# Banded attention and a top-1 mixture of experts in one program: loads, step order, routing order and the experts' branch are rearranged

## The chip, the core and the metric

The program runs on one core of one Trainium2 chip. A core has five engines with instruction queues of their own: PE multiplies matrices (its weight loads are shown as a row of their own, PEld), DVE, ACT and POOL do elementwise work, SP issues DMAs. Each runs its instructions in order; they wait for one another, and for transfers, by semaphores. Sixteen DMA engines move data between HBM and the core's SBUF, which has 128 partitions. The metric is device time in microseconds (us): the median over several runs of one execution of the whole program.

## What is computed

The inputs are q, k and v for 8 batches, 8 heads, 576 positions and 64 channels. Attention is banded: heads 0 to 3 see the last 32 positions, heads 4 to 7 see every fourth of the last 128. The result x (4608 tokens of 512) goes to a mixture of 8 experts, of which each token uses one:

```python
logits = x @ w_gate
e_idx = np.argmax(logits, axis=1)
gate_w = softmax(logits)[arange(N), e_idx]
eom = 1.0 / (1.0 + np.exp(-(x @ w_output_gate)))
for e in range(8):
    mask = e_idx == e
    h = np.maximum(x[mask] @ w1[e], 0.0)         # 512 -> 1024
    ye = h @ w2[e]                               # 1024 -> 512
    out[mask] = gate_w[mask, None] * eom[mask, e, None] * ye
```

How many tokens an expert gets is known only on the chip, once the logits are there.

## The kernel before

**Layout.** The positions of heads 4 to 7 are sorted by their rest modulo 4 on the host, so that both kinds of head see a band of 32 within blocks of 32. Two batches are one pair, a pair has nine steps, and a step works on 128 queries of all heads; there are 36 steps, g = 0 to 35. Buffers for q, k, v (`qb`, `kb`, `vb`) exist twice, for the even and the odd batch of a pair. `v2` is v moved on by one block, for the queries of even blocks. In `kb`, `vb` and `v2` the two heads that share a matmul lie in partitions 0 to 63 and 64 to 127, and zeros in the other half of each buffer keep them apart; the zeros are written once, by `clear`.

**One step.** `scores` adds the mask by a matmul and then 32 small matmuls into the PSUM tile `sp` (two buffers). `softmax` takes the maximum (L326), subtracts it (L330), both on DVE, takes exp on ACT (L336) and sums in halves on POOL (L341 to L347). `transpose_p` turns the weights on PE (L358) and ACT copies them to `pT` (L360). `values` multiplies by v (L370, 32 matmuls), `output` scales by the inverse sums into `x` on DVE (L392; four buffers) and SP writes `x` to the DRAM scratch `xs` in two or more DMAs (L402, L407). `transpose_x` turns `x` for the gate (L426) and ACT copies it to `xT` (L432, L435).

**Order.** The order on each engine is that of the program text (`manual_schedule`). Iteration g of the loop (L759) holds: transposed weights of step g-2, scores of g, x transposed of g-3, values of g-2, softmax of g, output of g-2. `load_qk` and `load_v` fetch the next pair's batches in pieces at fixed steps (table `loads`), all issued by SP, each to one half of the partitions; `v2` gets its upper 32 rows of each half by DMA (L285) and its lower 32 by a copy on DVE or ACT (`shift_v`, L290). Routing of a finished pair is spread over the next pair's steps by the tables `calm` and `brisk`: gate products, logits, argmax (`route_pick`), ranks, and one-hot matmuls into `perm`, from which come the lists of rows per expert.

**Experts.** Every expert has four 128-token tiles by default (`BASE`), expert 0 first three (`HEAD`), which are gathered from `xs` by indirect DMAs on POOL (L148; L162 in quarters). All values are split into a high and a low part of float32r, so that each product is three matmuls. Weights come as four 512 KB loads of each kind into the four `wraw` buffers (L110); ACT makes the high part (L128), DVE or POOL the low one (L132). For expert e the first products run over eight column blocks (`base_h`, L204, 12 matmuls each, then `relu` on ACT and DVE), the second over eight blocks and four tiles (`gemm2`, L835), then `finish` scales and scatters (L842 to L848). While expert 0's head runs, `during_first` and `during_second` do the last pair's routing. Tokens beyond four tiles are done after that, by one of five paths, chosen by a nest of compares of the count (`rest`, L1185 to L1193): nothing, up to 32 more, up to 128 more, up to 160 more, or two tiles more. In each path stands the second block of the next expert's first product (`fill`), as work for PE.

Of the kernel before, what the change touches and what calls it, by code (L numbers as in the profile page):

```python
# [7 lines left out]
F32 = mybir.dt.float32  # L8
# [7 lines left out]
PSUM = bass.MemoryType.PSUM  # L16

# [4 lines left out]
E = 8  # L22
# [24 lines left out]
def kernel(  # L47
# [21 lines left out]
    cnt = keep.tile([P, 2 * E + 3], I32, name="cnt")  # L69
# [155 lines left out]
    # ------------------------------------------------------------------ attention and routing  # L225
    with ExitStack() as actx:
# [30 lines left out]
        zeros = zero.broadcast_to([P, 2304])  # L257

        def clear(eng, t, c):
            r = slice(64 * (1 - c), 64 * (1 - c) + 64)  # L260
            v = t[r, c].rearrange("p a b -> p (a b)") if len(t.shape) == 4 else t[r, c].rearrange("p a b d -> p (a b d)")
            if eng is nc.scalar:
                eng.copy(out=v, in_=zeros[r])
            else:
                eng.memset(v, 0.0)

        def clear_first(z):
            for c in range(2):
                nc.gpsimd.memset(v2[z][64 * c + 32 : 64 * c + 64, c, :, 0], 0.0)

        def load_qk(b, j0, j1):
            z = b % 2
            nc.sync.dma_start(out=qb[z][:, :, 64 * j0 : 64 * j1], in_=qT[b, :, :, 64 * j0 : 64 * j1])
            for c in range(2):
                r = slice(64 * c, 64 * c + 64)
                nc.sync.dma_start(out=kb[z][r, c, j0:j1], in_=kT[b, r, j0:j1])

        def load_v(b, j0, j1):
            z = b % 2
            for c in range(2):  # L280
                r = slice(64 * c, 64 * c + 64)
                nc.sync.dma_start(out=vb[z][r, c, :, j0:j1], in_=vv[b, r, :, j0:j1])
                r = slice(64 * c + 32, 64 * c + 64)
                e1 = min(j1 + 1, 9)
                nc.sync.dma_start(out=v2[z][r, c, :, j0 + 1 : e1], in_=vv[b, r, :, j0 : e1 - 1])  # L285

        def shift_v(c, b, j0, j1):
            z = b % 2
            r = slice(64 * c, 64 * c + 32)
            (nc.vector.tensor_copy, nc.scalar.copy)[c](out=v2[z][r, c, :, j0:j1], in_=vb[z][r, c, :, j0:j1])  # L290
# [10 lines left out]

        def scores(g):
            var, subs = subs_of(g)
            sp = ps_s.tile([P, 512], F32, name="sp")
            nc.tensor.matmul(sp, lhsT=idb, rhs=mk[:, var], start=True, stop=False, skip_group_check=True)
# [15 lines left out]
            st[g, "s"] = sp  # L321

        def softmax(g):
# [7 lines left out]
                out=pt.rearrange("p (h k) -> p h k", h=H),  # L331
                in0=sp.rearrange("p (h k) -> p h k", h=H),
                in1=mx.unsqueeze(2).broadcast_to([P, H, 64]),
                op=ALU.subtract,
            )
            nc.scalar.activation(out=pt, in_=pt, func=AF.Exp, scale=1.0 / 8.0)  # L336
            sm = st[g, "sm"] = wk.tile([P, H], F32, name="sm", bufs=4)
            pv = pt.rearrange("p (h k) -> p h k", h=H)
            if g < last - 3 or g == last - 2:
                half = wk.tile([P, H, 32], F32, name="half", bufs=2)  # L340
                nc.gpsimd.tensor_tensor(out=half, in0=pv[:, :, 0:32], in1=pv[:, :, 32:64], op=ALU.add)  # L341
# [6 lines left out]
            st[g] = pt  # L348

        def late_sum(g):  # L350
            pv = st[g].rearrange("p (h k) -> p h k", h=H)
            nc.vector.tensor_reduce(out=st[g, "sm"], in_=pv, axis=AX.X, op=ALU.add)
# [33 lines left out]
        def output(g):  # L386
# [4 lines left out]
            x = wk.tile([P, DM], F32, name="x", bufs=4)  # L391
# [28 lines left out]
        def transpose_x(g):  # L420
# [7 lines left out]
            for p0 in range(0, P, n):  # L428
                b, i = subs[p0 // 32]
                o = (b % 2) * S  # L430
                s0 = 32 * i
# [20 lines left out]
        def gate_logits(pr, parts=(0, 4, 8)):  # L452
            lts = st[pr, "lt"]
            for c0 in parts:
                if c0 == 0:
                    R["spare"] = lts[0]
                    R["lg"] = rt.tile([P, NSTEP, 16], F32, name="lg")
# [917 lines left out]
```

## Time and profile before

| | |
|---|---|
| median of 3 runs | 714.92 us (713.82 to 715.13) |
| span of the profiled execution | 711.3 us |
| PE, DVE, ACT, POOL busy | 597.4, 351.5, 261.1, 372.3 us |
| mean granted TensorE clock | 0.940 |
| moved by DMA | 96.76 MB in 55784 packets |

The runs' time holds what lies around the span of the profile: 714.92 less 711.3 is 3.6 us. Attention takes the span up to some 204 us, expert 0 up to some 288, the other seven the rest. Busy time of an engine is the union of its instructions; DMA share is the mean busy share of the sixteen DMA engines, and can read above 1 where packets of one engine overlap. A row of a group has its busy time, the mean of one instruction, and the idle time of the engine before these instructions with what ended it.

### The profile page before, as it was taken

To read this page: it belongs to the slowest core of one execution; us is meant where nothing else is said; L and a number is where in the kernel's file an instruction comes from. 1 tells how busy PE (TensorE), PEld (TensorE's weight loads), DVE (VectorE), ACT (ScalarE), POOL (GpSimd) and SP (SyncE) were. 2 spreads that over 40 slices of the span, in tenths; PEclk is the share of its full clock that TensorE was granted. 3 is DMA by queue.
4 is the path that set the end of the run, shared out by engine and by line. 5 is a ranking of instruction groups with operands and counts; after the bars stand their busy time and mean duration, and the time that the engine had idled before them with its cause. 6 is when DMAs were issued, how large, how long until landed. Compare 5 with 4: busy or idle time off the path is not lost. (4 is left out here: it accounts for less than half of the span.)

```text
span 711.3 us, 13438 instructions
## 1 busy us (share of the span) xinstructions
PE 597.4 (84%) x5077; PEld 476.4 (67%) x5109; DVE 351.5 (49%) x620; ACT 261.1 (37%) x449; POOL 372.3 (52%) x497
## 2 busy tenths in 40 slices
PE   5685877877677799998599999499999959989992
PEld 4464655655456789786488788388778748858891
DVE  5453476594796574364175164256237417526020
ACT  4464555545563322343153243143234214324010
POOL 7753446474474376476475177277247647525110
PEclk8998998998899799999799999899999979999997
DMA  8999899889945342154155144244205415511010
GB/s 203 217 257 213 195 237 242 220 198 228 265 109 178 98 146 77 50 158 146 44 162 159 37 141 134 99 135 144 89 23 173 138 47 159 157 45 30 16 46 30
DMA packets 55784, 96.76 MB, mean 136 GB/s; under 512 B 10107, under 2 KB 40317, under 8 KB 55680
## 3 DMA queue, kind: packets, MB, share of 16 engines
q1 hardware_dynamic: 46800, 76.44, 40.8%
q0 software_dynamic: 8880, 18.91, 8.3%
q8 instruction: 68, 1.11, 0.7%
q14 instruction: 36, 0.29, 0.2%
HBM read 79.57 MB, written 19.27 MB: 139 GB/s over the span
## 5 line engine op out<-in xcount | busy, mean ns | idle before, releaser
L162 POOL DMA_INDIRECT sd<-xs,idx x112 | 130.4, 1164 | 34.0 <-issue 31.8
L204 PE MATMUL ph<-sc,w 128*128 128x512 f32 x480 | 115.8, 399 | 20.6 <-issue 17.4
L204 PEld LDWEIGHTS ph<-sc,w 128*128 128x128 f32 x480 | 91.6, 193 | 43.9 <-issue 20.6
L848 POOL DMA_INDIRECT out_dram<-yt,idx x39 | 38.6, 990 | 98.9 <-ACT yt L844 52.7
L162 POOL DMA_INDIRECT xg<-xs,idx x56 | 60.8, 1086 | 47.6 <-PE ph L204 22.6
L341 POOL TENSOR_TENSOR half<-pt 128x256 f32<-128x256 f32 x34 | 26.1, 767 | 67.4 <-ACT pt L336 67.0
L835 PE MATMUL y<-w,h 128*128 128x512 f32 x190 | 53.7, 390 | 0.0
L210 ACT ACTIVATE h<-ph 128x512 fp32r<-128x512 f32 (+1 forms) x48 | 28.1, 586 | 67.1 <-PE ph L204 62.1
L211 DVE SCALAR_TENSOR_TENSOR h<-ph,h 128x512 fp32r<-128x512 f32 (+1 forms) x48 | 32.3, 675 | 37.0 <-ACT h L210 36.9
L345 POOL TENSOR_TENSOR half<-half 128x128 f32<-128x128 f32 (+3 forms) x136 | 43.2, 318 | 10.7
L132 DVE TENSOR_TENSOR w<-wraw,w 128x1024 fp32r<-128x1024 f32 x36 | 44.0, 1227 | 8.1 <-ACT w L128 8.1
L392 DVE TENSOR_TENSOR x<-av,rs 128x512 f32<-128x512 f32 x36 | 24.8, 688 | 45.1 <-DMA xs<-x 23.8
L191 ACT CAST sc<-sd 128x512 fp32r<-128x512 f32 x28 | 17.4, 620 | 75.6 <-DVE sd L184 60.5
L204 PE MATMUL ph<-sc,sa 128*128 128x512 f32 (+1 forms) x132 | 35.8, 408 | 9.3 <-issue 8.2
L835 PE MATMUL z<-w,h 128*128 128x512 f32 x152 | 43.5, 389 | 0.0
L128 ACT CAST w<-wraw 128x1024 fp32r<-128x1024 f32 x40 | 41.6, 1044 | 0.0
L835 PEld LDWEIGHTS y<-w,h 128*128 128x128 f32 x190 | 35.5, 188 | 7.3
L370 PE MATMUL av<-sc,pT 128*32 128x128 f32 x288 | 26.7, 312 | 15.5 <-ACT pT L360 7.2
L426 PE MATMUL tp<-idn,x 128*128 128x128 f32 x144 | 24.3, 293 | 17.3 <-DVE x L392 15.0
L204 PEld LDWEIGHTS ph<-sc,sa 128*128 128x128 f32 x132 | 26.1, 205 | 14.4 <-issue 8.7
L326 DVE TENSOR_REDUCE mx<-sp 128x8 f32<-128x512 f32 x36 | 23.8, 662 | 21.6 <-PE sp L313 21.6
L426 PEld LDWEIGHTS tp<-idn,x 128*128 128x128 f32 x144 | 15.8, 145 | 27.9 <-DVE x L392 14.3
(284 smaller groups left out, 1344.5 us busy)
## 6 DMA issues: line engine op xcount, KB each, us to landing
wraw<-in_w_dram SPq DMA_DIRECT2D x64, 512.0 KB, 4.3
xs<-x SPq DMA_DIRECT2D x40, 128.0 KB, 5.8
vb<-in_vv_dram SPq DMA_DIRECT2D x8, 448.0 KB, 6.4
qb<-in_qT_dram SPq DMA_DIRECT2D x3, 896.0 KB, 9.8
kb<-in_kT_dram SPq DMA_DIRECT2D x6, 448.0 KB, 10.6
sb<-in_vv_dram SPq DMA_DIRECT2D x8, 320.0 KB, 5.0
sd<-in_qT_dram SPq DMA_DIRECT2D x4, 512.0 KB, 7.8
sa<-in_kT_dram SPq DMA_DIRECT2D x8, 256.0 KB, 6.9
```

Of the source, the lines that this page charges most:

```text
L128: nc.scalar.copy(out=W[e, kind][0][c], in_=raws[e, kind, c])
L132: sub.tensor_tensor(out=w[1][c], in0=raws.pop((e, kind, c)), in1=w[0][c], op=ALU.subtract)
L162: nc.gpsimd.indirect_dma_start(out=xg[j][:, P * a : P * a + P], out_offset=None, in_=xs4, in_offset=bass.IndirectOffsetOnAxis(ap=idx4[:, a ...
L204: nc.tensor.matmul(ph[:, 0:m], lhsT=part_of(w, a, o, P), rhs=x[:, c, 0:m], start=k == 0, stop=k == 3 * NC - 1)
L210: nc.scalar.activation(out=hh, in_=ph[:, 0:m], func=AF.Relu)
L211: nc.vector.scalar_tensor_tensor(out=hl, in0=ph[:, 0:m], scalar=0.0, in1=hh, op0=ALU.max, op1=ALU.subtract)
L341: nc.gpsimd.tensor_tensor(out=half, in0=pv[:, :, 0:32], in1=pv[:, :, 32:64], op=ALU.add)
L345: nc.gpsimd.tensor_tensor(out=dst, in0=half[:, :, 0:n], in1=half[:, :, n : 2 * n], op=ALU.add)
L370: nc.tensor.matmul(av[32 * a : 32 * a + 32, P * hp : P * hp + P], lhsT=pT[:, hp, 32 * a : 32 * a + 32], rhs=src[:, :, hp, i // 2, :], star ...
L426: nc.tensor.transpose(out=tp[:, c], in_=x[:, P * c : P * c + P], identity=idn)
L835: nc.tensor.matmul(y, lhsT=l[:, r], rhs=part_of(w, a, DM * fc, DM), start=fc == 0 and n == 0, stop=fc == NF - 1 and n == 2)
L848: put = nc.gpsimd.indirect_dma_start(out=out, out_offset=bass.IndirectOffsetOnAxis(ap=at.bitcast(U32), axis=0), in_=yt, in_offset=None, bo ...
```

## The change

**Attention, loads.** The two heads of a matmul now lie in alternate partitions: `lanes(c)` is every second partition, so that each DMA of 64 rows steps over all 128 partitions. Whole batches are loaded at once (`load_qk`, `load_vv`: 2 + 2 and 2 + 2 DMAs) instead of in pieces. The weights pt are kept in the matching interleaved order (`by_head`). `clear` now covers all 128 partitions, in two pieces for the first batch, and is left to DVE and POOL. For the first two pairs `v2` is made wholly on the core (`first_shift`: DVE one half of the partitions, ACT the other); for later pairs the upper half comes by DMA. At the start the first masks and k are issued by ACT, the rest by SP, cut to what the first steps need.

**Attention, order.** Iteration g now holds: transposed weights of g-2, mask of g, exp and sums of g-1, x transposed of g-4 (up to g = 27, then g-3), shifts, values and output of g-2, scores and maximum of g. Up to step 25 x lies in halves of the four `wraw` buffers (eight places), later in its own four. `transpose_x` copies in one piece, and the gate product reads the classes in strides (four products of 288 columns instead of 512, 512 and 128). The routing tables start earlier with the gates and end later. Ranks take 10 matmuls instead of 18, `route_spots` one instruction instead of nine. Low parts of expert 0's weights move from POOL to DVE.

**Experts.** In expert 0's head the last routing comes one block later, and its second weights are split on DVE in blocks 1 to 4. `choose` loads the number of an expert's path before its second product and announces the jump (`switch_hint`); the nest of compares becomes one jump through a table. Gathers go further ahead and are spread, the further tiles are prepared during the second product, two of each four blocks use other PSUM buffers, and the sums of a further tile lie in the tiles of the gathered rows, not in the output buffers.

```diff
+        def lanes(c, f0=0, f1=2):
+            return slice(64 * f0 + c, 64 * f1, 2)
+
+        def load_q(b, j0, j1):
             for c in range(2):
-                nc.gpsimd.memset(v2[z][64 * c + 32 : 64 * c + 64, c, :, 0], 0.0)
-
-        def load_qk(b, j0, j1):
+                s = slice(64 * j0, 64 * j1)
+                nc.sync.dma_start(out=qb[b % 2][lanes(c), :, s], in_=qT[b, rows_c(c), :, s])
+
+        def load_k(eng, b, j0, j1):
+            for c in range(2):
+                eng.dma_start(out=kb[b % 2][lanes(c), c, j0:j1], in_=kT[b, rows_c(c), j0:j1])
+
+        def load_qk(b):
+            load_q(b, 0, 9)
+            load_k(nc.sync, b, 0, 9)
+
+        def load_vv(b):
+            for c in range(2):
+                nc.sync.dma_start(out=vb[b % 2][lanes(c), c], in_=vv[b, rows_c(c)])
+                nc.sync.dma_start(out=v2[b % 2][lanes(c, 1), c, :, 1:9], in_=vv[b, rows_c(c, 1), :, 0:8])
+
+        def first_shift(f, b, j0, j1):
+            z = b % 2
+            j0, j1 = max(j0 - f, 0), j1 - f
+            r = slice(64 * f, 64 * f + 64)
             for c in range(2):
-                r = slice(64 * c, 64 * c + 64)
-                nc.sync.dma_start(out=kb[z][r, c, j0:j1], in_=kT[b, r, j0:j1])
+                (nc.vector.tensor_copy, nc.scalar.copy)[f](
+                    out=v2[z][r, c, :, j0 + f : j1 + f], in_=vb[z][r, c, :, j0:j1]
+                )
...
+            if g >= 26:
+                x = wk.tile([P, DM], F32, name="x", bufs=4)
+            else:
+                if g % 2 == 0:
+                    st["rows"] = stage.tile([P, 1024], F32, name="wraw")
+                x = st["rows"][:, DM * (g % 2) : DM * (g % 2) + DM]
...
+        load_k(nc.scalar, 0, 0, 2)
+        nc.scalar.activation(out=warm, in_=zero, func=AF.Exp)
...
+        loads = {4: 0, 8: 1}
...
         for g in range(last + 1):
             if g >= 2:
                 transpose_p(g - 2)
-                inverse(g - 2)
+            if g < last:
+                mask(g)
+            if g >= 1:
+                softmax(g - 1)
+            if 4 <= g <= hurry:
+                transpose_x(g - 4)
+            if g >= hurry:
+                transpose_x(g - 3)
             shift(1, g)
...
             if g >= 2:
                 values(g - 2)
-            routing(g, "ahead")
+                inverse(g - 2)
+                output(g - 2)
+                load(g - 2, load_vv if g > NSTEP + 2 else whole_v)
             if g < last:
-                softmax(g)
-            if g >= 2:
-                output(g - 2)
-                load(g - 2, load_v)
...
+                scores(g)
+                shifted(g)
...
+    def choose(e):
+        flag[e] = nc.values_load(cnt[0:1, 2 * E + 3 + e : 2 * E + 4 + e], min_val=0, max_val=len(PATHS))
+        flag[e, "hint"] = tc.switch_hint({t: flag[e] for t in ENGINES}, len(PATHS) + 1, f"paths{e}")
...
-        elif k == 1:
+        elif k == 2:
             rank_products(pr)
...
-            split_w(0, 1, k, nc.gpsimd)
+        if 0 < k < 5:
+            split_w(0, 1, k - 1)
...
+    for n in tc.Switch(flag["rare"], 2, flag["rare", "hint"]):
+        products1(1, 1, *X, BASE * P, ph, (1, 2, 3))
+        if n:
+            repair()
...
-            h.append(base_h(e, fc, X, BASE * P))
+            h.append(base_h(e, fc, X, BASE * P, ph=bank(ps_x, "tpx") if fc % 4 > 1 else None))
             if fc == 2:
-                gather4(e, 4)
-                gather4(e, 5)
-                next_gathers(e + 1)
+                rows_of(e + 1, *((2, 3) if e > 1 else range(BASE)))
+                rows_of(e, 4, 5)
...
-            if fc >= 6:
-                prep4(fc - 2, *xx, fc - 6)
+        choose(e)
...
+            if fc in (4, 5):
+                prep4(fc, *xx, fc - 4)
+            if fc == 5:
+                rows_of(e + 2, 0, 1)
...
-        rest([
-            ((BASE + 1) * P + 32, two),
-            ((BASE + 1) * P, lambda: extra(e, BASE, xx, 1, 1, fill)),
-            (BASE * P + 32, lambda: extra(e, BASE, xx, 1, 0, fill)),
-            (BASE * P, lambda: extra(e, BASE, xx, 0, 1, fill)),
-            (0, nothing),
-        ])
+        bodies = [
+            nothing,
+            lambda: extra(e, BASE, xx, 0, 1, fill),
+            lambda: extra(e, BASE, xx, 1, 0, fill),
+            lambda: extra(e, BASE, xx, 1, 1, fill),
+            two,
+        ]
+        for n in tc.Switch(flag[e], len(bodies), flag[e, "hint"]):
+            bodies[n]()
```

More of the change, by code (lines that the diff above doesn't have):

```diff
@@ L443, in gate_products @@
+                nc.scalar.copy(out=xT[:, :, o : o + n], in_=tp[:, :, p0 : p0 + n])
+        def gate_products(pr, parts=range(4)):
+            if (pr, "lt") not in st:
+                st[pr, "lt"] = rt.tile([P, 2 * S], F32, name="lt")
+            m = S // 2
+            for k in parts:
+                o = S * (k // 2)
+                i0 = m // NCLS * (k % 2)
                 gp = ps_t.tile([P, 512], F32, name="tp")
                 for c in range(NC):
+                    by_class = _free(xT, 2 * S * c + o + i0, [[1, m // NCLS], [CLS, NCLS]])
@@ L897, with rows_of @@
     pr = NPAIR - 1
-    def next_gathers(e):
+    def rows_of(e, *js):
         if e < E:
-            for j in range(BASE):
+            for j in js:
                 gather4(e, j)
```

343 lines of the change are left out of this document (176 added, 167 removed).

## The prediction

> **What bounds the kernel now.** I read the page first, then engine busy time by stage, then PE's waits in each stage, then the DMA rate in single stretches, then the branches.
>
> ```profile
> span 711.3 us, 13438 instructions
> DMA  8999899889945342154155144244205415511010
> ```
>
> Forty slices of 17.8 us: the DMA engines are at eight tenths and more in the first eleven, the attention, and mostly below five later. The stages, with columns us, then PE, PEld, DVE, ACT, POOL busy, PE clock, DMA share, GB/s:
>
> ```profile
> 0.00:204.00 204.00, 147.62 (x2759) 111.25 (x2791) 122.56 (x279) 104.88 (x210) 114.23 (x268) 0.91 0.94 223
> 204.00:288.00 84.00, 73.95 (x523) 63.81 (x524) 52.88 (x119) 28.22 (x54) 47.63 (x41) 0.94 0.35 112
> 288.00:711.00 423.00, 375.78 (x1796) 301.31 (x1794) 176.05 (x223) 128.03 (x186) 210.45 (x189) 0.96 0.32 99
> ```
>
> There are three limits. In attention PE is idle for 56.4 of 204 us while DMA is at 0.94: transfers set the pace. In the other two stages DMA is at a third, and PE is busy 73.95 of 84 and 375.78 of 423: PE sets the pace, and only its idle time can be won. What ends the waits in attention, for PE and then for DVE and ACT (us in total, times, longest):
>
> ```profile
> PE tp L426 <- DVE x L392: 12.9, 9, 2.7
> PE sp L313 <- DMA sa<-in_kT_dram: 6.3, 2, 5.6
> PE av L370 <- DMA sb<-in_vv_dram: 5.1, 1, 5.1
> DVE x L392 <- DMA xs<-x: 23.8, 9, 5.6
> ACT sc L290 <- DMA sb<-in_vv_dram: 21.1, 5, 7.6
> ```
>
> PE's longest wait is for x, and x waits for one of its four places, whose write to DRAM stands in the same queue as the loads. So this too is a transfer that is late.
>
> Why are the transfers slow at a share of 0.94? One stretch shows it. SP issued a q load (all 128 partitions), then the k pair (64 neighbouring partitions each), and the two stretches are those in which first q, then k moves; the third holds v loads, 64 neighbouring partitions too:
>
> ```profile
> 65.82 0.60 SPq L273 DMA_DIRECT2D qb<-in_qT_dram  x1
> 66.46 1.27 SPq L276 DMA_DIRECT2D kb<-in_kT_dram  x2
> ...
> 69.50:72.50 3.00, 2.64 (x40) 2.25 (x44) 0.63 (x2) 1.63 (x2) 2.44 (x8) 0.50 1.13 323
> 73.00:76.00 3.00, 2.86 (x48) 1.72 (x41) 1.08 (x2) 2.11 (x5) 0.04 (x1) 1.00 0.96 186
> 86.00:88.00 2.00, 1.85 (x40) 1.49 (x35) 1.47 (x5) 1.60 (x4) 1.00 (x2) 1.00 1.11 200
> ```
>
> With all DMA engines busy, q moves at 323 GB/s, k at 186, v at 200: a load into half of the partitions goes at some 0.6 of the rate.
>
> **Attention, transfers.** Per batch q, k and v have 1152 KB each and the upper half of v2 512 KB (64 rows of 4 x 8 x 64 floats). Over eight batches k, v and v2 are 23.1 MB; at 193 GB/s, between 186 and 200, that is 120 us of the DMA time, which is 0.94 x 204 = 192 us. q is 9.4 MB at 323, 29 us. The other 43 us are x, masks and expert 0's weights. The change steps every load over all 128 partitions and drops v2's load for four batches: 21.0 MB are left in place of 23.1. No row shows a load with a step between partitions. Below, its rate is that of half the partitions (193), above, that of q (323). I take q's, since a stepped load reaches from partition 0 to 127 as q does: 21.0 MB in 65 us, and 43 + 29 + 65 = 137 us in place of 192.
>
> The Trainium skill has this as a rule ("SBUF — State Buffer", section Door 1: The DMA port swizzle): 64 neighbouring partitions reach 8 of the 16 ports, about half of the bandwidth. The measured 186 to 200 against 323 agree. The same section says that only a transfer spanning all 128 partitions hits all ports; if "spanning" meant touching each of them, the lanes would gain nothing, and that is the first rival.
>
> **Attention, PE.** With transfers at 137, PE's 147.6 us are the longest sum, so PE becomes the bound. How full can PE get here? The fullest stretches of ten us, and a middling one:
>
> ```profile
> 80.00:90.00 10.00, 9.22 (x196) 7.44 (x198) 7.55 (x16) 5.08 (x12) 4.81 (x14) 1.00 0.76 164
> 170.00:180.00 10.00, 8.76 (x189) 7.22 (x183) 5.91 (x16) 2.30 (x5) 2.43 (x8) 1.00 0.69 176
> ```
>
> Where DMA is at 0.7 to 0.8, PE is busy for 0.88 to 0.92. I take the lower: 147.6 / 0.88 = 168 us, 36 less than 204; bounds 0.92 (160, a gain of 44) and 0.80 (184, a gain of 20). The reordering is costed inside this term: x one step later and with eight places takes away the 23.8 and the 12.9, exp of the step before takes ACT's and DVE's time off the way to the next scores. Its cover is gone if another engine exceeds PE, so I add up DVE and ACT from these rows (a shift on each; the subtraction that writes pt; the one-hot rows; a low part on DVE; x's copies and a copy of a whole tile on ACT):
>
> ```profile
> L290 DVE COPY sc<-sb x8: 671/744/1508, 17.3 to 166.1; 32x1024 f32<-32x1024 f32 x4, 32x1280 f32<-32x1280 f32 x4
> L290 ACT COPY sc<-sb x8: 1041/1148/1255, 18.5 to 164.4; 32x1024 f32<-32x1024 f32 x4, 32x1280 f32<-32x1280 f32 x4
> L330 DVE TENSOR_TENSOR pt<-sp,mx 128x512 f32<-128x512 f32 x36 | 24.9, 692 | 3.1
> L567 DVE TENSOR_SCALAR ohp<-cb,pos 128x128 bf16<-128x128 bf16 x36 | 12.5, 417 | 0.0
> L132 DVE TENSOR_TENSOR w<-wraw,w 128x1024 fp32r<-128x1024 f32 x36 | 44.0, 1227 | 8.1 <-ACT w L128 8.1
> L435 ACT COPY xT<-tp 128x256 f32<-128x256 f32 (+7 forms) x64 | 24.1, 444 | 0.0
> L432 ACT COPY xT<-tp 128x256 f32<-128x256 f32 (+1 forms) x40 | 14.4, 359 | 17.8 <-PE tp L426 17.3
> L360 ACT COPY pT<-tp 128x512 f32<-128x512 f32 x36 | 20.8, 578 | 10.5 <-PE tp L358 10.2
> ```
>
> A batch's shift is two such copies per engine. DVE: four batches with twice the shift, + 4 x 1.5; two batches given to ACT, - 2 x 1.5; three times nine one-hot rows (27 x 0.417 = 11.3) become three instructions of up to 3.8, no gain below and 11 above, I take - 5; three low parts from POOL, + 3.7. That is 122.6 + 2 = 124 of 168. ACT: 24.1 + 14.4 become 40 copies of 0.58, - 15; shifts + 4 x 2.3 and + 2 x 2.3, + 14; at the start the k and mask DMAs in ACT's queue (0.6 each, eight) replace its three clears. So ACT stays near 105. Each stays under PE, but in single steps with routing DVE will not (its mean is 124 / 36 = 3.4 us a step, PE's 147.6 / 36 = 4.1); the step of slack that x gets takes such a burst. The interleaved write of pt and the strided read of the gate product have no row; at nothing they cost 0, at twice the time (L330's group is 24.9 us, all on DVE) DVE would reach 149 and stand beside PE. I take 0, since the same elements are read.
>
> **Expert 0.** What PE waits for between 204 and 288:
>
> ```profile
> PE tp L504 <- DVE oh L495: 4.0, 1, 4.0
> PE perm L573 <- DVE ohp L567: 3.4, 2, 2.1
> PE tp L426 <- DVE x L392: 2.1, 1, 2.1
> PE tp L176 <- DVE sc L180: 1.7, 1, 1.7
> ```
>
> That is 11.2 us. Ranks one block later put 12 more matmuls (some 2.3 us by the blocks' pace) ahead of the 4.0; fewer one-hot instructions shorten the way to the 3.4, but three of the four low parts at 1.23 now stand on DVE in front of it. Neither of the other two is touched. I take - 5, between 0 and - 9.
>
> **Experts 1 to 7.** PE's waits after 288, the branch instructions of the nest, and one of the three long waits:
>
> ```profile
> PE ph L204 <- issue: 25.6, 3, 9.2
> PE ph L204 <- ACT sc L191: 3.2, 3, 1.3
> PE y L1053 <- DMA out_dram<-yt,idx: 1.9, 1, 1.9
> PE y L1043 <- ACT sa L210: 1.6, 1, 1.6
> PE ph L204 <- DVE sc L192: 0.7, 3, 0.2
> ...
> L1190 PEldq COMPARE_BRANCH  x26: 70/340/4714, 334.6 to 692.7; - x26
> L1190 ACTq COMPARE_BRANCH  x26: 38/45/55, 337.6 to 697.1; - x26
> ...
> 334.09 2.81 PE L204 MATMUL ph<-sc,w 128*128 128x512 f32 x11 [0.22 <-DVE sc L192]
> 346.06 0.79 PE L204 MATMUL ph<-sc,w 128*128 128x512 f32 x1 [9.16 <-issue]
> ```
>
> Three experts have no further tokens and pass the whole nest; there PE stands still for 25.6 us, waiting for nothing but its own sequencer, since its branches take up to 4.7 us and ACT's 0.05. A long one costs between 9.16 / 3 = 3.1 and 4.7. One jump in place of four compares removes 25.6. If it is announced in time it costs what a short branch does, 0.07 to 0.34, under the 2.81 of queued matmuls. If not, up to 4.7 once on entering and once on leaving, less the same cover: up to 1.9 each. I take 0.4 for each of seven experts, 3 in all. On the other engines, whose branches are short now, the table could bring such jumps: at most 9.4 us after each expert's output. Behind them wait the next relu and low parts; PE has four blocks of twelve matmuls (some 2.9 each, 11 in all) before it needs a PSUM buffer back, as two more buffers are used. So: nothing, and with that cover gone up to 6 us each. The 1.9 and 1.6 are waits for output buffers and for an ACT sum in further tiles, which now lie elsewhere: I take both off. In sum - 25.6 - 3.5 + 3 = - 26.
>
> Here the skill ("Runtime: NRT & Kernel Launch", section Instruction fetch mechanics) says that a taken branch out of a small window of 256-instruction blocks forces a fetch, and it knows no announcement. The 4.7 on PE against 0.05 on ACT agrees; by that rule alone the jump would stay a fetch, which is the second rival.
>
> The start of the next expert waits 3.2 + 0.7 for rows' preparation, late because 24 gathers stand in a row on POOL. They are spread and the further tiles' eight go behind the next expert's: - 3.5, between 0 and - 3.9.
>
> **Sum.** 711.3 - 36 - 5 - 26 - 3.5 = 640.8. The runs' median stands 3.6 above the span, so 644.4.
>
> **Rivals.** First, the stepped loads are no faster: 43 + 29 + 21.0 MB / 193 (109) = 181, at the same share of 0.94 it is 193 us, a gain of 11 in place of 36: 669. For it: no row has such a step. Against it: 323 beside 186 within seven us of the trace. Second, the announcement doesn't help: 1.9 twice on the seven, less the 3 counted, + 12 at most by half covers, + 24 with none of it hidden: 656 to 668. With both, 681. Third, slower than before: the stepped loads are slower than those into neighbours, q among them, which loses its full load. All loads are then 30.4 MB, and the other terms give back 34.5; the kernel is slower once (43 + 30.4 MB / rate) / 0.94 exceeds 238.5, which is from 168 GB/s down. At 150 it is 43 + 203 = 246, a stage of 261: 711.3 + 57 - 34.5 + 3.6 = 737. For it: q's two DMAs now have half of the rows each. Against it: no full stretch above is under 186, and whole batches make longer rows.
>
> **How the numbers follow.** Forecast 0.62 (own range 630 to 660), first rival 0.16, second 0.14, third 0.05, anything that leaves no difference 0.01, other mishaps 0.02 that still are faster. The range reaches down to 628 (PE at 0.92, 9 in expert 0) and up to 678, so that the first two rivals and nearly their sum are in. A measurement here tells 0.2% from nothing, that is 1.4 us. Faster 0.94, same 0.01, slower 0.05.
>
> **What will show it.** k loads at 300 GB/s and more with DMA full; the last scores starting before 170 us; PE's waits for x and DVE's for xs gone; no PE wait "issue" above 2 us after 288; PE near 0.9 busy in attention. The forecast is wrong if attention still has DMA at 0.94, or if DVE's busy share there passes PE's.

## The result and the profile after

The changed kernel takes 629.45 us (median, 626.08 to 631.82) against 714.75 us before (713.82 to 715.13), a ratio of 0.8803 with the interval 0.8767 to 0.8839. The forecast was 644.4, with an own range of 630 to 660; the measured time lies just below that and inside the whole range of 628 to 678. The profiled execution took 631.7 us and has a span of 629.9.

From the page after: the span, the engines' busy time, and the row of 40 slices (now 15.7 us each) for the granted clock.

```profile
span 629.9 us, 13742 instructions
PE 580.8 (92%) x5084; PEld 468.2 (74%) x5109; DVE 353.2 (56%) x621; ACT 256.6 (41%) x416; POOL 364.9 (58%) x488
PEclk9889999999999999999999999999999999999995
```

The same two rows for PE and its clock from the page before:

```profile
PE 597.4 (84%) x5077; PEld 476.4 (67%) x5109; DVE 351.5 (49%) x620; ACT 261.1 (37%) x449; POOL 372.3 (52%) x497
PEclk8998998998899799999799999899999979999997
```

PE does nearly the same matmuls (5077 and 5084 records, and 5109 weight loads in both), yet it is busy for 16.6 us less. The clock row goes with it: before, it has a 7 or an 8 at several places all along the span; after, it has hardly one behind the third slice. The forecast had held PE's work constant.

Engine busy time by stage shows both parts. Columns: us, then PE, PEld, DVE, ACT, POOL busy, PE clock, DMA share, GB/s. First before: attention, head of expert 0, experts 1 to 7, and then one of the three long waits, cut into the wait, the time behind it and the time after that.

```profile
0.00:211.50 211.50, 152.99 (x2848) 115.44 (x2880) 129.25 (x287) 110.63 (x222) 120.68 (x273) 0.91 0.91 217
211.50:265.00 53.50, 45.59 (x295) 38.82 (x291) 35.45 (x90) 16.56 (x30) 27.22 (x21) 0.90 0.43 139
288.00:697.00 409.00, 375.71 (x1796) 301.31 (x1794) 176.05 (x223) 127.34 (x185) 209.46 (x188) 0.97 0.33 102
337.00:346.00 9.00, 0.00 (x0) 0.00 (x0) 0.69 (x1) 0.59 (x1) 1.78 (x2) 0.62 0.25 91
346.00:349.30 3.30, 3.24 (x8) 2.56 (x9) 0.00 (x0) 0.00 (x0) 1.86 (x2) 0.50 0.10 25
349.30:353.00 3.70, 3.70 (x18) 3.05 (x17) 0.69 (x1) 0.60 (x1) 2.79 (x4) 0.99 0.13 35
```

Then after: the same three stages, and a stretch in which a stepped k load moves.

```profile
0.00:176.00 176.00, 148.54 (x2871) 115.38 (x2896) 134.06 (x288) 106.16 (x192) 119.31 (x268) 0.97 0.79 249
176.00:218.90 42.90, 41.19 (x279) 34.64 (x275) 33.11 (x90) 16.06 (x26) 18.04 (x17) 1.00 0.52 169
241.00:614.00 373.00, 368.86 (x1799) 297.92 (x1797) 175.53 (x223) 128.08 (x185) 212.50 (x189) 1.00 0.36 114
53.00:56.00 3.00, 2.93 (x70) 2.55 (x73) 2.46 (x6) 2.62 (x6) 1.67 (x4) 1.00 1.00 346
```

Behind the wait of 9 us PE works for 3.3 us at a clock of 0.50: eight matmuls where the next 3.7 us hold eighteen. Such a stall costs its length and some of the work behind it. The two parts by stage, from these rows (idle is the stretch less PE's busy time):

| | PE idle | PE busy |
|---|---|---|
| attention | 58.5 to 27.5, -31.0 | -4.5 |
| expert 0's head | 7.9 to 1.7, -6.2 | -4.4 |
| experts 1 to 7 | 33.3 to 4.1, -29.2 | -6.9 |

That is 66.4 us of idle time and 15.7 us of busy time. By exact bounds (first product of expert 0, of its two further tiles, of expert 1, last matmul) the stages went from 211.5, 53.5, 22.8, 409.3 and 14.2 us to 176.0, 42.9, 22.5, 372.8 and 15.7. These stage times are used for all experiments below. One execution of each kernel was profiled: in the six profiles whose attention is as changed it takes 170.1 to 176.0 us, the kernel after being the longest, so differences of up to 6 us in that stage say little.

What PE still waits for in attention after (us in total, times, longest), and what DVE waits for:

```profile
PE tp L461 <- DVE x L427: 6.0, 5, 2.0
PE sp L336 <- issue: 4.1, 2, 2.7
...
DVE wraw L427 <- PE av L400: 7.9, 4, 5.9
DVE rs L414 <- POOL sm L378: 7.6, 9, 1.4
```

DVE's 23.8 us for a place of x are gone, and of ACT's 21.1 for the v loads into `sb` 5.0 are left. The rest is spread over many short waits. In experts 1 to 7 no wait of PE is above 1.2:

```profile
PE tpx L206 <- DVE el L213: 1.2, 1, 1.2
...
PE tpx L206 <- issue: 0.8, 1, 0.8
```

### The profile page after: what moved, and what is told of

Read it like the earlier page. It is cut to its first block, busy times and chain, and to the rows that moved or that the text cites. A ratio compares the mean times of both kernels' runs of the same rounds, so it can differ in the third digit from the quotient of the medians.

```text
span 629.9 us, 13742 instructions
## 1 busy us (share of the span) xinstructions
PE 580.8 (92%) x5084; PEld 468.2 (74%) x5109; DVE 353.2 (56%) x621; ACT 256.6 (41%) x416; POOL 364.9 (58%) x488
## 3 DMA queue, kind: packets, MB, share of 16 engines
q1 hardware_dynamic: 30352, 72.90, 36.5%
## 5 line engine op out<-in xcount | busy, mean ns | idle before, releaser
L206 PE MATMUL tpx<-sc,w 128*128 128x512 f32 x240 | 56.7, 391 | 2.7 <-DVEq L1285 1.0
L206 PE MATMUL ph<-sc,w 128*128 128x512 f32 x240 | 57.6, 391 | 0.0
L206 PEld LDWEIGHTS tpx<-sc,w 128*128 128x128 f32 x240 | 44.7, 188 | 13.6 <-PE ph L206 2.6
L206 PEld LDWEIGHTS ph<-sc,w 128*128 128x128 f32 x240 | 44.7, 188 | 10.7 <-issue 1.7
L370 POOL TENSOR_TENSOR half<-pt 128x256 f32<-128x256 f32 x34 | 29.5, 868 | 27.3 <-ACT pt L365 26.4
L899 PEld LDWEIGHTS y<-w,h 128*128 128x128 f32 x190 | 35.4, 188 | 9.1 <-issue 1.8
L193 ACT CAST sc<-sd 128x512 fp32r<-128x512 f32 x28 | 17.4, 621 | 52.3 <-issue 33.3
L213 DVE SCALAR_TENSOR_TENSOR h<-tpx,h 128x512 fp32r<-128x512 f32 x28 | 19.3, 691 | 26.1 <-ACT h L212 26.1
L899 PEld LDWEIGHTS z<-w,h 128*128 128x128 f32 x152 | 28.5, 188 | 5.9
L365 ACT ACTIVATE pt<-pt 128x512 f32<-128x512 f32 x36 | 22.7, 631 | 24.6 <-DVE pt L355 15.5
L212 ACT ACTIVATE h<-tpx 128x512 fp32r<-128x512 f32 x28 | 16.8, 599 | 38.0 <-PE tpx L206 35.6
L194 DVE TENSOR_TENSOR sc<-sd,sc 128x512 fp32r<-128x512 f32 x28 | 19.4, 693 | 20.3 <-ACT sc L193 20.3
L390 ACT COPY pT<-tp 128x512 f32<-128x512 f32 x36 | 21.1, 587 | 18.5 <-PE tp L388 18.4
```

The source lines that it names most:

```text
L194: nc.vector.tensor_tensor(out=view(xl[:, :, r]), in0=tv, in1=view(xh[:, :, r]), op=ALU.subtract)
L206: nc.tensor.matmul(ph[:, 0:m], lhsT=part_of(w, a, o, P), rhs=x[:, c, 0:m], start=k == 0, stop=k == 3 * NC - 1)
L213: nc.vector.scalar_tensor_tensor(out=hl, in0=ph[:, 0:m], scalar=0.0, in1=hh, op0=ALU.max, op1=ALU.subtract)
L370: nc.gpsimd.tensor_tensor(out=half.rearrange("p (h c) k -> p h c k", c=2), in0=pv[:, :, :, 0:32], in1=pv[:, :, :, 32:64], op=ALU.add)
L390: nc.scalar.copy(out=pT, in_=tp)
L899: nc.tensor.matmul(y, lhsT=l[:, r], rhs=part_of(w, a, DM * fc, DM), start=fc == 0 and n == 0, stop=fc == NF - 1 and n == 2)
```

## The experiments

Theory A behind the forecast, now with the clock added: attention was paced by loads at some 0.6 of the rate, the experts by the nest's branches, and each long idle stretch also costs PE some work at half the clock. The rivals are named at each run. Unless said otherwise an edit is made to the changed kernel.

### The nest of compares back

```diff
-        flag[e, "hint"] = tc.switch_hint({t: flag[e] for t in ENGINES}, len(PATHS) + 1, f"paths{e}")
...
-        for n in tc.Switch(flag[e], len(bodies), flag[e, "hint"]):
-            bodies[n]()
+        def rest(n):
+            if n == 0:
+                bodies[0]()
+                return
+            with tc.If(flag[e] > n - 1) as more:
+                bodies[n]()
+            with more.Else():
+                rest(n - 1)
+        rest(len(bodies) - 1)
```

> The changed kernel, with the nest of compares in place of the announced jump. In the trace of the kernel before, PE stood idle 25.6 + 1.9 + 1.6 us after its branches, and half-clock windows lay over the time after each of the three long ones. Theory A (idle time and the clock after it): the 29 us come back and some 5 us more of PE time at half clock, time 660 to 665, three half-clock windows among the experts. Theory B (idle time alone, as the prediction had it): 26 us, time 655 to 658, clock among the experts as now.

Measured: 664.63 us (661.87 to 665.26), ratio 0.9309 (0.9272 to 0.9345). The experts' stage takes 408.2 us, 35.4 more than in the changed kernel. Its row, PE's first waits in it, and the nest's branches on PE (count, then shortest, median and longest in ns):

```profile
238.00:646.00 408.00, 380.21 (x1797) 304.95 (x1795) 175.76 (x223) 127.63 (x185) 209.06 (x188) 0.96 0.33 102
...
PE ph L206 <- issue: 18.7, 3, 6.6
PE y L1129 <- issue: 4.0, 2, 3.2
...
L1289 PEldq COMPARE_BRANCH  x26: 70/3094/3832, 281.6 to 641.8; - x26
```

Idle time is 27.8 us against 4.1, so 23.7 more, and PE's busy time is 11.4 higher at a clock of 0.96: 35.1 in sum. The nest alone thus carries nearly the whole gain of this stage (36.5), and a third of that is clock. Theory A had the total, but with more idle time (29) and less of the clock (5). What the rows of the next experts and the buffers gave, costed at 3.5 each in the forecast, this run does not separate: its stage is only 1.1 us shorter than that of the kernel before, with 5.5 us less idle time and 4.5 more of busy time.

### The jump without its announcement

```diff
-        flag[e, "hint"] = tc.switch_hint({t: flag[e] for t in ENGINES}, len(PATHS) + 1, f"paths{e}")
...
-        for n in tc.Switch(flag[e], len(bodies), flag[e, "hint"]):
+        for n in tc.Switch(flag[e], len(bodies)):
```

> The jump through the table stays, its announcement goes (for experts 1 to 7). Theory A (the announcement brings the code in time): PE is held up at each jump by a fetch of 3.1 to 4.7 us less some 2.8 us of queued matmuls, on entering and perhaps on leaving: 8 to 24 us more, 637 to 653. Theory B (one jump instead of four compares is the whole gain): no more than 2 us longer than the changed kernel, 628 to 632.

Measured: 628.53 us (627.73 to 630.46), ratio 0.8809 (0.8771 to 0.8847): no difference from the changed kernel. PE's jumps with the announcement, and then without it:

```profile
L1448 PEldq COMPARE_BRANCH  x16: 293/320/4100, 241.0 to 609.9; - x16
```

```profile
L1447 PEldq COMPARE_BRANCH  x16: 309/2382/3992, 236.4 to 605.9; - x16
...
236.00:609.00 373.00, 368.54 (x1797) 298.05 (x1796) 175.26 (x223) 127.36 (x185) 212.35 (x189) 1.00 0.36 114
```

The announcement shortens some jumps: the median takes 0.32 us and not 2.38, though five of the sixteen still take 3.4 to 4.1 us with it, and eight take 3.3 to 4.0 without. But PE's idle time is the same (4.5 without, 4.1 with, of 373), since one such jump lies under matmuls that are already queued: PE's longest wait behind one is 1.1 us. What cost 9 us before was three long branches in a row (3.88, 3.56 and 3.42 us inside the wait of 9.16). The Trainium skill ("Runtime: NRT & Kernel Launch", section Instruction fetch mechanics) says that a jump out of the instruction window forces a fetch. The unannounced jumps of 3.3 to 4.0 us fit that, and here they cost nothing.

### q and k into halves of the partitions again

```diff
-                nc.sync.dma_start(out=qb[b % 2][lanes(c), :, s], in_=qT[b, rows_c(c), :, s])
+                nc.sync.dma_start(out=qb[b % 2][rows_c(c), :, s], in_=qT[b, rows_c(c), :, s])
...
-                eng.dma_start(out=kb[b % 2][lanes(c), c, j0:j1], in_=kT[b, rows_c(c), j0:j1])
+                eng.dma_start(out=kb[b % 2][rows_c(c), c, j0:j1], in_=kT[b, rows_c(c), j0:j1])
```

> Only q and k are loaded into halves of neighbouring partitions again, two loads each; v, its copies and the whole order stay. Theory A (the step over all partitions gives the rate): k at some 190 GB/s in full stretches, 18.9 MB of q and k take 98 us of DMA time and not 58, DMA share in attention back above 0.9, attention 11 to 20 us longer, 640 to 650. Theory B (the order of steps and the eight places for x did it): 628 to 634, with DMA share up but PE's waits as now.

Measured: 651.72 us (648.59 to 654.48), ratio 0.9133 (0.9079 to 0.9187), 22.3 us more, slightly above what A gave. In the profiled execution attention takes 193.7 us, 17.7 more, with the DMA engines at 0.90. The second row is a full stretch with q and k in it:

```profile
0.00:185.00 185.00, 145.08 (x2770) 112.54 (x2795) 126.27 (x275) 99.75 (x181) 113.10 (x261) 0.95 0.90 231
62.00:69.00 7.00, 5.59 (x145) 4.57 (x145) 6.51 (x14) 5.64 (x9) 4.39 (x9) 1.00 1.02 229
```

The same bytes in the same DMAs, only without the step between partitions, move slower: 229 GB/s against the 346 of the profile after. Whole batches alone thus take the rate from 186 to some 229, and the step does the rest. (q is slowed here too, which the kernel before loaded at 323.) The Trainium skill ("SBUF — State Buffer", section "Can I just issue two DMAs to hit both halves?") wants one transfer to span all 128 partitions to hit all ports. The 346 GB/s of the stepped k load show that every second partition is enough. The first rival falls.

### A row of idle times, empty and filled

Ahead of five experts' second products PE is made to wait for 1, 3, 5, 8 or 12 copies of a tile by ACT on itself. No value changes.

```diff
+        if e in DELAY:                      # {1: 1, 2: 3, 3: 5, 4: 8, 5: 12}
+            scr = next_yt()
+            nc.scalar.copy(out=scr, in_=h[NF - 1][0])
+            for _ in range(DELAY[e]):
+                nc.scalar.copy(out=scr, in_=scr)
+            nc.tensor.transpose(out=ys[0][:, 0:P], in_=scr[:, 0:P], identity=idn)
```

> Ahead of the second product of experts 1 to 5 PE waits for a chain of copies on ACT, 2, 4, 6, 9 and 13 copies of 0.58 us, about 2.2, 3.3, 4.5, 6.2 and 8.5 us of idle time, 25 us in all; nothing else changes. Theory A (idle time brings a slower clock after it): from some length on each idle stretch is followed by a half-clock window that takes 3 to 5 us of PE's work at half speed, 1.5 to 2.5 us lost each, time 658 to 666. Theory B (the clock does not follow idle time): 25 us, 652 to 656, with no half-clock windows among the experts.

The second version has the same delays, but PE is given 9, 14, 20, 28 or 40 matmuls meanwhile, whose products are overwritten.

```diff
+            for _ in range(DELAY[e][1]):
+                nc.tensor.matmul(ys[1], lhsT=h[0][0][:, 0:P], rhs=part_of(W[e, 1], 0, 0, DM), start=True, stop=True)
```

> The five delays of the run before it, with PE multiplying throw-away products (9, 14, 20, 28 and 40 matmuls of 512 columns, some 0.24 us each) while it would have waited. The delays themselves were 27.3 us of idle time and the experts' stage 38.0 us longer. Theory A (idle time brings the half clock): no half-clock window among the experts, the stage 27 to 30 us longer than in the changed kernel, time 655 to 660. Theory B (the windows come with the chain's own delay, or by chance): 38 us as before, 664 to 668.

Measured: 664.59 us (663.09 to 665.72; ratio 0.9307, 0.9267 to 0.9348) with the waits empty, 657.2 (655.92 to 659.18; ratio 0.922, 0.9188 to 0.9251) with them filled. The experts' stage grew by 38.0 us empty and 28.5 filled. With empty waits, first the stretch behind each of the five, in order, then the whole stage, then PE's waits that were put in:

```profile
261.20:265.00 3.80, 3.80 (x18) 3.13 (x19) 2.25 (x3) 1.89 (x3) 2.98 (x3) 1.00 0.30 70
308.70:314.60 5.90, 5.90 (x15) 4.64 (x16) 4.14 (x5) 2.36 (x3) 4.89 (x4) 0.50 0.39 127
372.10:376.10 4.00, 4.00 (x10) 3.20 (x11) 2.45 (x3) 2.09 (x3) 3.22 (x3) 0.50 0.21 50
425.00:430.70 5.70, 5.70 (x14) 4.47 (x15) 3.96 (x5) 2.33 (x3) 1.11 (x2) 0.50 0.27 92
501.10:505.80 4.70, 4.70 (x12) 3.73 (x13) 2.96 (x4) 2.34 (x3) 0.40 (x1) 0.50 0.31 99
...
235.00:646.00 411.00, 380.19 (x1804) 305.00 (x1802) 175.67 (x223) 148.81 (x219) 208.15 (x189) 0.96 0.33 103
...
PE y L1257 <- issue: 21.5, 3, 9.8
PE y L1257 <- ACT yt L1256: 5.8, 2, 3.6
```

The same stage with the waits filled:

```profile
237.60:638.80 401.20, 395.63 (x1913) 318.46 (x1911) 175.56 (x223) 149.00 (x219) 206.34 (x189) 1.00 0.33 106
```

The two shortest waits are 3.6 and 5.8 - 3.6 = 2.2 us. Behind 2.2 the clock is 1.00; behind 3.6 and every longer one it is 0.50, for 4.0 to 5.9 us of work, however long the wait was. At half clock half of that work is lost: (5.9 + 4.0 + 5.7 + 4.7) / 2 = 10.2 us, and PE's busy time is 380.19 - 368.86 = 11.3 higher. With PE kept at work in the same waits the clock stays at 1.00 and the stage is 9.5 us shorter. This shows the clock as a cost of its own. The length of a wait alone does not settle it, though. In the profile after, a stretch of 2.0 us without matmuls and weight loads in attention is followed by work at 0.50 (first two rows), and in the run with the nest 5.2 us of a wait of 5.65 pass at 1.00 (third):

```profile
105.50:107.50 2.00, 0.00 (x0) 0.00 (x0) 1.44 (x4) 0.54 (x1) 0.77 (x4) 1.00 0.53 166
108.10:111.40 3.30, 3.08 (x18) 2.33 (x12) 0.00 (x0) 1.66 (x4) 0.17 (x1) 0.50 0.84 247
515.90:521.10 5.20, 0.00 (x0) 0.00 (x0) 0.69 (x1) 0.59 (x1) 2.77 (x3) 1.00 0.30 105
```

The Trainium skill ("TensorE: Matmul & The Clock Gate", section Part 1: The HAM clock gate) gives some 3.4 us of idle time for the halving and some 3.4 of work for the return. The first lies between the 2.2 and 3.6 us of the planted waits, but the stretches of 2.0 and 5.2 us do not fit it as a fixed length; for the return the rows have 4.0 to 5.9, and 3.3 after the wait shown of before.

### The rate without the order, and the order without the rate

The kernel before, with only q and k stepped over the partitions (and the zeros of the k buffers with them):

```diff
-            nc.sync.dma_start(out=qb[z][:, :, 64 * j0 : 64 * j1], in_=qT[b, :, :, 64 * j0 : 64 * j1])
             for c in range(2):
                 r = slice(64 * c, 64 * c + 64)
-                nc.sync.dma_start(out=kb[z][r, c, j0:j1], in_=kT[b, r, j0:j1])
+                nc.sync.dma_start(out=qb[z][c:P:2, :, 64 * j0 : 64 * j1], in_=qT[b, r, :, 64 * j0 : 64 * j1])
+            for c in range(2):
+                r = slice(64 * c, 64 * c + 64)
+                nc.sync.dma_start(out=kb[z][c:P:2, c, j0:j1], in_=kT[b, r, j0:j1])
```

> One part of the change alone, put into the kernel before: q and k step over all partitions (two loads each, in the old pieces), and k's buffers are cleared whole at the start; order, places for x, v and experts as before. Theory A (the rate of the loads sets the pace of attention): 18.9 MB at the rate of a full load, up to 40 us less DMA time, of which 12 to 25 us are seen, 690 to 703. Theory B (the old order cannot use it, since x waits for its places and its turn): less than 6 us, 708 to 714.

Measured: 705.23 us (703.24 to 710.66), ratio 0.9892 (0.9864 to 0.992). Attention takes 199.1 us, 12.4 less than before, and the experts 3.7 more. Neither theory's bounds hold it. Theory A's gain was too high from the start: q moved at 323 GB/s already, so that only k's rate rises. The stage, and ACT's waits for loads in it:

```profile
0.00:191.00 191.00, 153.08 (x2838) 112.68 (x2839) 125.30 (x281) 106.54 (x216) 116.25 (x271) 0.94 0.91 239
...
ACT sc L294 <- DMA sb<-in_vv_dram: 17.3, 5, 7.4
ACT v L294 <- DMA vb<-in_vv_dram: 17.0, 5, 4.7
```

The v loads, still into half of the partitions, are the largest waits for loads that are left: ACT stands idle 34.3 us for them (39.5 before), and DVE still 13.0 for a place of x. That the v loads hold the stage back is read from these waits; no run stepped v in the old order.

Then the changed kernel with all loads into neighbouring partitions (and the shifts, zeros and the order of pt fitted to that):

```diff
-            return slice(64 * f0 + c, 64 * f1, 2)
+            return slice(64 * c + 32 * f0, 64 * c + 32 * f1)
...
-            return pt.rearrange("p (h k c) -> p h c k", h=4, c=2)
+            return pt.rearrange("p (h c k) -> p h c k", h=4, c=2)
```

> The changed kernel with q, k, v and v2 all loaded into halves of neighbouring partitions, whole batches and the new order kept, v2's zeros cleared at the start. q and k alone made it 22 us longer. Theory A (the rate of the loads is what attention gained; the new order by itself adds little): another 11.5 MB at 193 and not 340 GB/s, up to 26 us more DMA time, attention's stage at 205 to 215 us as in the kernel before, time 660 to 672. Theory B (the order and the whole loads carry a part of 10 us and more by themselves): the stage stays under 200 us, 650 to 658.

Measured: 721.72 us (708.58 to 731.75). It ran, like two others below, on a chip on which the kernel before itself took 750.18 us, so its time says little; on that chip PE pauses between the dense products of the experts. Expert 0's two further tiles, which no edit touches, in this run and then in the changed kernel on its own chip:

```profile
248.90:287.00 38.10, 27.41 (x145) 24.53 (x146) 10.60 (x21) 5.46 (x12) 14.27 (x15) 0.78 0.14 46
```

```profile
218.90:241.40 22.50, 22.50 (x145) 20.61 (x146) 10.48 (x21) 5.57 (x12) 14.45 (x15) 1.00 0.23 78
```

Attention isn't slower there: two other runs on that chip have 175.4 us (attention as changed) and 174.4 in place of 176.0. So attention is read, and it takes 206.1:

```profile
0.00:197.00 197.00, 153.03 (x2790) 117.75 (x2795) 131.53 (x274) 104.49 (x182) 113.93 (x263) 0.90 0.93 218
```

The DMA engines are at 0.93 again. The four kernels give attention times of 211.5 (neither), 206.1 (order alone), 199.1 (rate of k alone) and 176.0 (both); with q and k slow in the new order it was 193.7. On top of the order v's rate is worth 12.4 us and that of q and k 17.7, both well over the spread of 6. The 5.4 us of the order alone lie within it, and there q too goes into halves: its 9.4 MB at 229 in place of 323 GB/s are an estimated 12 us of DMA time. So in the new order the loads make 30.1 us of difference, a part of it by q, which is no gain over the kernel before. What the order is worth with q at its old rate, and whether the old order could have used v's rate, no run shows.

### Eight places and the fourth step for x

```diff
-            if g >= 26:
+            if g >= 0:
                 x = wk.tile([P, DM], F32, name="x", bufs=4)
```

> The changed kernel with x in four buffers of its own all the way, not in eight halves of the weights' buffers. Theory A (with fast loads x's writes land in time): within 3 us, 627 to 633. Theory B (the places are needed, whole batches stand ahead of x's writes in the queue): DVE waits for x's writes again, 5 to 15 us more, 635 to 645.

Measured: 630.08 us (626.8 to 632.35), ratio 0.8843 (0.8811 to 0.8875), attention 171.0. Then x transposed three steps behind throughout:

```diff
-        hurry = 27
+        hurry = 3
...
-            if 4 <= g <= hurry:
+            if 4 <= g < hurry:
```

> The changed kernel with x transposed three steps behind in the whole loop, not four up to step 27. Theory A (the step of slack takes DVE's late x off PE's way): PE's waits for x come back, some 5 to 12 us more, 634 to 641. Theory B (eight places and fast loads did it, the step is not needed): within 3 us, 627 to 633.

Measured: 627.91 us (625.16 to 633.78), ratio 0.8814 (0.8753 to 0.8874), attention 174.4. Neither shows a gain once the loads are fast: both stages lie within the spread, and so do the times. With four places DVE's waits in attention begin with the first of these, and only the last is for a place whose write is under way:

```profile
DVE rs L414 <- POOL sm L378: 7.1, 8, 1.4
...
DVE x L427 <- DMA xs<-x: 0.2, 1, 0.2
```

So the 23.8 and 12.9 us of before were, as far as this shows, the slow loads seen from another place: x's write stood behind them in the queue.

### Expert 0's head, put back step by step

The last routing one block earlier, as before, and the second weights' low parts on POOL again:

```diff
-        elif k == 2:
+        elif k == 1:
             rank_products(pr)
...
-        if 0 < k < 5:
-            split_w(0, 1, k - 1)
+        if k < 4:
+            split_w(0, 1, k, nc.gpsimd)
```

> The changed kernel with expert 0's head as before: ranks one block earlier, low parts of the second weights on POOL in blocks 0 to 3, lists of rows one block earlier, scale and counts in the old places. The head took 53.5 us before and 42.9 after. Theory A (the place of routing in the head): the waits for one-hot rows come back, 6 us, with the half clock behind them, 4 us: head at 50 to 54 us, time 636 to 642. Theory B (the head gained from what came earlier, fewer one-hot instructions and an attention that ends in order): head at 43 to 46 us, 628 to 633.

Measured: 682.99 us (671.42 to 689.78) on the chip just told of, where the ratio is unclear. The head, whose time is read, has 44.5 us against 42.9, and 42.8 and 43.9 in the other two runs on that chip: at most 1.7 of the gain of 10.6, hardly clear of that spread. Then, with that edit kept, the last pair's gate products all moved behind the loop of steps:

```diff
-            if g in (last - 1, last):
-                gate_products(NPAIR - 1, (g - last + 1,))
...
-        gate_products(NPAIR - 1, (2, 3))
+        gate_products(NPAIR - 1, range(4))
```

> The run before it with routing in the head as before (head 44.5 us), and with it the last pair's first two gate products back behind the loop (8 matmuls of 288 columns each, 2.3 us of PE work that thereby moves from the stage of attention to the head). Theory A (the early gates make DVE's argmax early enough for the ranks): PE's wait for the argmax grows to 3 to 5 us with half clock behind it, head at 50 to 54 us. Theory B (the wait was shortened by DVE's smaller load, one instruction for the one-hot rows of a pair): head at 46 to 48.5 us, the moved work and little else.

Measured: 635.74 us (633.13 to 638.46), ratio 0.8892 (0.8817 to 0.8966), on an undisturbed chip. The head has 49.7, just under what A gave, and 5.2 more than in the run before; some 2.3 of these are the two gate products themselves, which now stand in the head. PE's longest wait in the head, in the run before this one and then in this:

```profile
PE tp L544 <- DVE oh L535: 1.8, 1, 1.8
```

```profile
PE tp L544 <- DVE oh L535: 4.0, 1, 4.0
```

The wait of 4.0 us of the kernel before is back. Two of the four gate products done inside the loop take 2.2 us off it; the later ranks, with what else the run before put back, the other 1.8. The 3.8 us that are left to 53.5 were not tried by themselves; the waits for one-hot rows (3.4 in the forecast's fence) are gone in all these kernels, whose one-hot rows are made by one instruction.

### Low parts on POOL, masks in one load

```diff
-                split_lo(0, 0, g - 33, nc.vector)
+                split_lo(0, 0, g - 33, nc.gpsimd)
...
-        nc.scalar.dma_start(out=mk[:, 0:1], in_=cmask[:, 0:1])
+        nc.scalar.dma_start(out=mk[:, 0:2], in_=cmask[:, 0:2])
```

> An attempt to better the changed kernel: expert 0's three low parts in the loop go back from DVE to POOL, where PE's waits for x in the last steps (6.0 us) come from a full DVE, and the second mask is loaded with the first, ahead of k (2.1 us of waiting). Theory A (those waits are on the path): 3 to 6 us less, 623 to 627. Theory B (the waits move to the next late operand): within 2 us, 627 to 632.

Measured: 693.76 us (687.42 to 704.05) on the disturbed chip. Attention takes 174.4 us against 175.4 on that chip: no gain that stands clear of the spread. PE still waits for x:

```profile
PE tp L461 <- DVE x L427: 5.4, 4, 2.6
```

No version that was tried is clearly faster than the changed kernel; without the announcement, with four places or with three steps it is the same.

## Why the prediction was right, and where it was off

**Direction, bound and mechanism.** They held. The limits were read rightly: attention was paced by loads, the experts by PE's idle time. What the sum lacked is the clock. The forecast had 15.0 us too much. Of the spans' difference, 640.8 - 629.9 = 10.9, the head has 5.6 and experts 1 to 7 have 7.0; attention was short by 0.5, the further tiles gave 0.3 and the tail took 1.5. The other 4.1 are in "what lies around": 3.6 were added, but the execution profiled after lies 1.8 above its span and 2.25 above its median, so most of that is spread between executions.

**Attention, transfers.** 137 us of DMA time were forecast; 0.79 x 176 = 139 were there. The choice of q's rate was right: 346 GB/s.

**Attention, PE.** 36 us forecast, 35.5 measured, but so close by luck: by two errors that cancel, in a stage that spreads over 6 us. PE's sum was taken as constant and fell from 152.99 to 148.54, and it fills 148.54 / 176 = 0.84 of the stage, not 0.88. Many short waits make up the rest. The crediting of x's lag and places inside this term was wrong too: neither shows a gain.

**What was costed at nothing.** The interleaved write of pt was to cost 0, with 24.9 us as the bound. Its group after, then the one-hot rows, forecast at up to 3.8 us each, then the gate product before and after, whose strided read was to cost 0 too:

```profile
L355 DVE TENSOR_TENSOR pt<-sp,mx 128x512 f32<-128x512 f32 x36 | 24.9, 693 | 3.6 <-ACT pT L390 0.5
...
L602 DVE TENSOR_TENSOR ohp<-cb,pos x4: 1340/1385/1431, 96.4 to 196.3; 128x1152 bf16<-128x1152 bf16 x4
...
L445 PE MATMUL tp<-xT,wgt 128*32 128x512 f32 (+1 forms) x96 | 10.8, 554 | 0.0
L478 PE MATMUL tp<-xT,wgt 128*32 128x288 f32 x128 | 19.3, 541 | 1.6 <-issue 1.6
```

The first is unchanged from 24.9. The second gives 3 x 1.39 = 4.2 in place of 11.3, a gain of 7.1 where 5 was taken in all. The gate product was not free: the same columns keep PE busy for 19.3 us and no longer 10.8, most of it in attention, where PE has become the bound. Whether the strides do it or the shorter products is not shown; no run put the old form back. Over the whole stage DVE is busy for 134.06 us (129.25 before, 2 more forecast) and ACT for 106.16 (110.63 before, no change forecast).

**Expert 0.** -5 was the term; -10.6 came, just past its bound of -9. Idle time gave 6.2, inside the bounds. The failing step is that a wait was priced at its length: PE's busy time fell by 4.4 as well, with the clock at 1.00 and no longer 0.90. And the end of the longest wait was put down to the later ranks alone; more of it came from the earlier gate products.

**Experts 1 to 7.** -29.5 was the sum of the branches and the starts; idle time fell by 29.2. The 6.9 us of busy time are the missing term. Within the sum, the 3 us for announced jumps were not needed, and the close agreement in idle time is in part luck: the nest put back brings only 23.7 us of it.

**Rivals.** Stepped loads at half the rate, or slower: refuted. An announcement that doesn't help: half true. It brings nothing measurable, but the price of 12 to 24 us was wrong, since the cover of queued matmuls holds one fetch whole; the forecast had reckoned with 2.81 us of it.

**The signs named.** k at 300 GB/s and more, the last scores before 170 us (they start at 166.3), no wait "issue" above 2 us in the experts: seen. PE near 0.9 in attention and no wait for x: not seen (0.84, 6.0 us).

## What to carry to other kernels

Price a stall that is taken away at its length, plus, where it is longer than some 2 to 5 us, half of the 3 to 6 us of matmuls behind it that run at half the clock; the rows of the clock beside a stage's busy time show whether that is so. A load of half the rows is worth stepping over all partitions where the loads pace a stage. Look at places and lags after that, since those waits may be the same loads seen from behind. Several long branches in a row cost PE dearly, one of up to 4 us cost nothing here under queued matmuls. An instruction that reads the same elements with strides is not free until a row shows it.

## What the hardware showed that was not expected

A planted idle stretch of 2.2 us left PE's clock alone, one of 3.6 halved it; elsewhere a stretch of 2.0 us was followed by half the clock, and 5.2 us of another passed at full clock. The work at half clock behind the planted waits (4.0 to 5.9 us) did not grow with the wait up to 9.8 us. A 64-row DMA with a step of two partitions ran at 346 GB/s, one into 64 neighbours with rows as long at some 229. And one chip ran dense products with pauses: 38.1 us for two tiles that took 22.5 on the others, PE busy for 27.4 of it, at a DMA share of 0.14; its cause stays open.
